# A fused attention and gated-MLP kernel: the second tile's keys loaded in halves, integers compared without a cast, zero products on TensorE before its register loads

## The chip, the cores and the metric

The kernel runs on one core of one Trainium2 chip. The time is device microseconds of one execution. Each run gives the time of the whole execution, and one profiled execution gives a trace whose span is a little shorter than that execution's time. The engines are TensorE (PE, with PEld for its weight loads), VectorE (DVE), ScalarE (ACT), GpSimd (POOL) and SyncE (SP, which here only issues DMAs). A name with a q (PEldq, SPq) is an engine's sequencer.

## The reference

```python
# attention: batch 2, 8 heads, 768 positions, 64 values a head; n_global = 8, n_local = 96
scores = scale * np.matmul(q, k.transpose(0, 1, 3, 2))
rel = pos[:, None] - pos[None, :]
is_global = pos[None, :] < int(n_global)
is_local = (rel >= 0) & (rel < int(n_local))
keep = is_global | is_local
dist = np.where(is_global & ~is_local, float(n_local), np.abs(rel))
scores = np.where(keep, scores - slopes[:, None, None] * dist, -1e9)
a = softmax(scores);  x = np.matmul(a, v)          # then (B, S, 512)
# first gated block: causal convolution of 5 taps as the gate
gate = sigmoid(conv(x, conv_w));  x = (gate * (x @ w_val)) @ w_out
# second gated block: width 1024, centred convolution of 3 taps as the gate
h = relu(x @ w_in);  out = (h * sigmoid(conv(h, conv_w2))) @ w_out2
```

`n_global` and `n_local` are 64-bit integers in memory. `w_out` of the first block and `w_in` of the second are multiplied once, on TensorE, and used as one matrix.

## The kernel before, in words

The queries are worked through in 12 tiles of 128 (two batches of six). A tile's scores are taken against its own 128 keys and the 128 before it, in whose unused columns the global keys are copied. Per tile TensorE makes the scores (line 461) in two halves, heads 0 to 3 and heads 4 to 7; each half uses two of four score banks, so a tile's first half needs the banks that the first half of the tile before it has left, and its second half those of the other half. DVE adds the bias and finds the least value of each head ("least", line 472, one instruction and one short read of the accumulator per head); ACT takes the exponential (line 477); POOL and DVE scale by the reciprocal of the sum (lines 488 to 501); TensorE transposes the result by the identity ("turn", line 528) into the single bank `t`, ACT or DVE copies it out (lines 532 and 538), and TensorE multiplies by the values (line 553). The weights come in 64-bit form through `raw` buffers and are rebuilt as 32-bit numbers by ACT, POOL and DVE (lines 262 to 272); their products and the gated blocks follow, beside the later attention tiles and after them.

The work within the two arms of a branch is planned ahead: a list scheduler (`Plan`) with costs and ring buffers writes out the order of each engine, and the engines keep to it. What stands before the branch is written by hand, in `attention_gated_mlps` (lines 852 to 864): the integers `li`, the first tile's keys and queries `k0` (two halves, one on ACT's queue, one on SP's) and its values `v0` are loaded; every engine loads the integers from memory into its own registers (line 860); DVE turns `li` into floats (`lf`, line 371) and makes the first mask from them (lines 374 to 376). The registers decide the branch of line 957; the arm for small windows is the one that runs. The first things in that arm are the first tile's scores on TensorE, the biases `b` of the eight heads on DVE and POOL (lines 383 and 385), and on SP the load of the second tile's keys and queries (`kq`, 512 KB, line 434). SP's DMA issues stand in one queue, eight DMAs may be under way before an issue waits for an earlier one to land, and each load after the first few waits for its buffer.

Of the kernel before, what the change touches and what calls it, by code (L numbers as in the profile page):

```python
# [9 lines left out]
F32 = mybir.dt.float32  # L10
# [5 lines left out]
PSUM = bass.MemoryType.PSUM  # L16

P = 128
NB, NH, S, D = 2, 8, 768, 64
DM = NH * D  # L20
DFF = 1024
NPAIR = NH // 2
# [5 lines left out]
GW = 32  # L28
# [11 lines left out]
RAWS, MBUFS, HBUFS, Z2BUFS, PBUFS, PTBUFS, KQBUFS, VBUFS = 3, 2, 6, 3, 11, 4, 3, 4  # L40
EARLY = -5.0
LANDING = 2.4
# [184 lines left out]
def dma_us(kb):  # L227
    return max(0.4, kb / 385.0)
# [121 lines left out]
def scratch(c):  # L350

    x = [c.x[:, d, XP:] for d in range(NC1)]
    c.rel, c.w, c.d = (x[d][:, 0:WIN] for d in range(3))
    c.key, c.far, c.d0 = (x[d][:, 4 * P : 5 * P] for d in range(3))


def positions(c):

    nc = c.nc
    nc.gpsimd.iota(c.rel, pattern=[[-1, WIN]], base=P, channel_multiplier=1, allow_small_or_imprecise_dtypes=True)  # L360
    nc.gpsimd.iota(c.key, pattern=[[1, P]], base=0, channel_multiplier=0, allow_small_or_imprecise_dtypes=True)
    nc.gpsimd.affine_select(
        out=c.rel, in_=c.rel, compare_op=ALU.is_ge, fill=BIG, base=P, pattern=[[-1, WIN]], channel_multiplier=1
    )


def first_mask(c):

    nc = c.nc
    lf = c.small.tile([P, 2], F32, name="lf")  # L370
    nc.vector.tensor_copy(lf, c.li[:, :, 0])
    c.ng, c.nl = ng, nl = lf[:, 0:1], lf[:, 1:2]
    rel, w = c.rel[:, P:], c.w[:, P:]
    nc.vector.tensor_scalar(c.far, c.key, ng, BIG, ALU.is_ge, ALU.mult)
    nc.vector.scalar_tensor_tensor(w, rel, nl, c.far, ALU.is_ge, ALU.mult)
    nc.vector.scalar_tensor_tensor(c.d0, rel, nl, w, ALU.min, ALU.add)
# [29 lines left out]
        pl.any(head_ways(c, WIN, lambda h=h: c.B[:, h, :], d, h), [], ["d"], [("B", h)])  # L406


def fast_attention(c, ap):

    nc, ident, pl = c.nc, c.ident, c.plan
# [3 lines left out]
    def tiles_of(tag, shape, n):  # L415
        return pl.ring(n, lambda: ap.tile(shape, F32, tag=tag, bufs=n, name=tag))

    kqr, vr = tiles_of("kq", [P, NPAIR, 2, P], KQBUFS), tiles_of("v", [P, 2, 4, D], VBUFS)
    pr_, ptr, sts = tiles_of("p", [P, WIN], PBUFS), tiles_of("pts", [P, 2, 2, P], PTBUFS), tiles_of("st", [P, 3, NH], 3)
    gl = ap.tile([P, NPAIR, GW], F32, name="gl")  # L420
    kq, vs = {}, {}

    def keys(t, pr, what):
        return c.first[0][:, pr, what] if t == 0 else kq[t].t[:, pr, what]

    def vals(t, h):
        return c.first[1][:, h // 2, h % 2] if t == 0 else vs[t].t[:, h // 4, h % 4]
# [1 line left out]
    def load(t):  # L429
        b, i = tiles[t]  # L430
        if t == 0:
            return
        kq[t], vs[t] = kqr.new(), vr.new()
        pl.add("SP", dma_us(512), lambda: nc.sync.dma_start(kq[t].t, c.kq[b, i]), [kq[t]], [], [("kq", t)], delay=LANDING)
        src = c.v[b, i * P : (i + 1) * P].rearrange("s h d -> s (h d)")
        pl.add(
            "SP", dma_us(256), lambda: nc.sync.dma_start(vs[t].t.rearrange("p a h d -> p (a h d)"), src),
            [vs[t]], [], [("v", t)], delay=LANDING,
        )
# [4 lines left out]
    for t in range(nt):  # L444
        b, i = tiles[t]
# [3 lines left out]
        nk = len(js) * P  # L449
        st, p = sts.new(), {}  # L450
        load(t)
        for half in range(2):
            s = [c.ring["s"].new() for z in range(2)]

            def scores(half=half, s=s, js=js, t0=t):
                for pr in (2 * half, 2 * half + 1):
                    for n, j in enumerate(js):
                        for z in range(2):
                            hs = slice(z * D, (z + 1) * D)
                            out = s[z].t.rearrange("p (a w) -> p a w", w=WIN)[:, pr % 2, n * P : (n + 1) * P]  # L460
                            nc.tensor.matmul(out, keys(t0, pr, 1)[hs], keys(j, pr, 0)[hs], start=True, stop=True)  # L461
# [44 lines left out]
                )  # L506

        def first_keys(t=t, i=i):
            r = (c.first[0] if t == 0 else kq[t].t)[:, :, 0, 0:GW]
            a, z = (gl, r) if i == 0 else (r, gl)  # L510
            nc.gpsimd.tensor_scalar(a, z, 1.0, 1.0, ALU.mult, ALU.mult)

        if i == 0:
            pl.add("POOL", 0.4, first_keys, held(kq, [t]), [("kq", t)], ["gl"])
        elif i < NT - 1:
            pl.add("POOL", 0.4, first_keys, held(kq, [t]), ["gl"], [("kq", t)])
# [315 lines left out]
def attention_gated_mlps(ctx, tc, kq, v, nn, w_val, conv_w, w_out, w_in2, w_out2, out):  # L832
    nc = tc.nc
    c = Ctx()
# [11 lines left out]
    k0 = c.x[:, :, XP + 2 * P : XP + 4 * P].rearrange("p n (t s) -> p n t s", t=2)  # L846
    v0 = c.x[:, :, XP + 5 * P : XP + 6 * P].rearrange("p a (h d) -> p a h d", d=D)
    c.first = k0, v0
    c.li = c.small.tile([P, 2, 2], I32, name="li")
    one = c.small.tile([P, 1], F32, name="one")  # L850
    c.ident = c.const.tile([P, P], F32, name="ident")
    with tc.manual_schedule():
        nc.sync.dma_start(c.li.rearrange("p n t -> p (n t)"), c.nn.to_broadcast([P, 4]))
        nc.scalar.dma_start(k0[:, 0:2], kq[0, 0, :, 0:2])
        nc.sync.dma_start(k0[:, 2:4], kq[0, 0, :, 2:4])
        nc.scalar.dma_start(v0, v[0, 0:P].rearrange("s (a h) d -> s a h d", a=4))
        scratch(c)
        positions(c)
        nc.vector.memset(one, 0.0)
        _, (glo, ghi, llo, lhi) = nc.values_load_multi_w_load_instructions(c.nn)  # L860
        nc.scalar.activation(one, one, AF.Exp)
        nc.gpsimd.memset(c.x[:, :, 0:XP], 0.0)
        make_identity(nc, c.ident)
        first_mask(c)
# [9 lines left out]
    def arm(fast):  # L874
        with ExitStack() as es:
# [42 lines left out]
            if fast:  # L918
                masks(c, ap)
                attention = fast_attention(c, ap)  # L920
                next(attention)
                n0 = len(pl.work)
# [78 lines left out]
```

## Time and profile before

| | |
|---|---|
| median of 3 runs | 288.72 us (288.35 to 290.06) |
| the profiled execution's own time | 289.12 us |
| its span in the trace | 286.9 us |
| TensorE, DVE, ACT, POOL busy | 94%, 83%, 65%, 33% of the span |
| first product of TensorE | 4.88 us after the span's start |

The busy shares are means over the whole span. The change touches its first part, so the timeline of the first 20 us is read on its own. A row of the timeline gives the start, the duration, the engine, the line, the tiles, and in brackets how long the engine had been idle and what released it. A product of 32-bit numbers on TensorE shows as two instructions, so a count of 16 there is eight products.

### The profile page before, as it was taken

The page shows a single profiled execution, that of the slowest core. Times are in us where ns is not written, and L with a number is a line of the kernel's source. Part 1 is how long each engine was busy: PE and PEld are TensorE (multiplying, and loading weights), DVE is VectorE, ACT ScalarE, POOL GpSimd, SP SyncE. Part 2 cuts the span into 40 slices and gives each one's busy share as a digit, 9 for nine tenths or more (in the row PEclk, how much of TensorE's full clock was granted, in tenths as well). Part 3 has the DMA queues.
Part 4 walks back from the last instruction along what each step waited for, and adds up shares of the span by engine and source line. Part 5 has one row for each costly group of instructions (what it writes and reads, how often), then busy time and mean ns, then how long its engine had stood idle before and what let it go on. Part 6 is the DMA issues. An engine that isn't in the chain of part 4 may idle for free.

```text
span 286.9 us, 5416 instructions
## 1 busy us (share of the span) xinstructions
PE 270.1 (94%) x1832; PEld 227.9 (79%) x1832; DVE 238.6 (83%) x607; ACT 187.2 (65%) x468; POOL 95.4 (33%) x208
## 2 busy tenths in 40 slices
PE   2689799999999999999999999999999999999993
PEld 2567556564557998999999999988999988899882
DVE  3899999999999999999899999999985654356600
ACT  2899798967677879775688554894464354445510
POOL 4555557445554405563443310320512000003000
PEclk9999999999999999999999999999999999999999
DMA  4985756645634111023510000010000011000112
GB/s 133 344 322 143 239 197 213 251 138 169 216 108 148 48 65 58 9 75 93 170 43 0 2 0 0 1 39 38 37 2 0 0 73 39 37 0 2 39 73 85
DMA packets 10276, 26.17 MB, mean 91 GB/s; under 512 B 1408, under 2 KB 2688, under 8 KB 10240
## 3 DMA queue, kind: packets, MB, share of 16 engines
q1 hardware_dynamic: 9440, 25.22, 26.3%
q10 hardware_dynamic: 800, 0.52, 0.6%
q8 instruction: 16, 0.26, 0.4%
q14 instruction: 20, 0.16, 0.2%
HBM read 22.59 MB, written 3.15 MB: 90 GB/s over the span
## 4 chain that ended last, share of the span: by engine, by line
PE 73%; DVE 15%; POOL 3%; issue 3%; ACT 3%; POOLq 1%; DVEq 0%; ACTq 0%
PE s L244 8%; PE s L245 8%; PE s L243 8%; PE f L243 7%; PE f L245 7%; PE f L244 7%; PE s L461 4%; PE x L553 4%; PE t L528 4%; DVE p L472 3%; DVE z L671 2%; PE t L243 2%; PE t L245 2%; PE x L245 2%; PE x L244 2%
## 5 line engine op out<-in xcount | busy, mean ns | idle before, releaser
L477 ACT ACTIVATE p<-p,st 128x256 f32<-128x256 f32 (+1 forms) x96 | 46.1, 483 | 8.0 <-DVE st L472 6.4
L671 DVE SCALAR_TENSOR_TENSOR z<-h,cw,z 128x384 f32<-128x384 f32 x64 | 39.9, 630 | 12.6 <-ACT z L666 10.9
L673 ACT ACTIVATE z<-z 128x384 f32<-128x384 f32 (+2 forms) x48 | 25.2, 524 | 26.2 <-DVE z L671 25.5
L671 DVE SCALAR_TENSOR_TENSOR z<-x,cw,z 128x400 f32<-128x400 f32 (+1 forms) x64 | 39.6, 643 | 0.2
L244 PE MATMUL s<-w,g 128*128 128x512 f32 (+1 forms) x104 | 39.2, 377 | 0.0
L245 PE MATMUL s<-w,g 128*128 128x512 f32 (+1 forms) x104 | 39.2, 377 | 0.0
L243 PE MATMUL s<-w,g 128*128 128x512 f32 (+1 forms) x104 | 39.1, 376 | 0.0
L501 POOL TENSOR_SCALAR p<-p,st 128x256 f32<-128x256 f32 (+1 forms) x50 | 32.5, 660 | 11.0 <-DVE st L491 8.7
L528 PEld LDWEIGHTS t<-ident,p 128*128 128x128 f32 x176 | 19.8, 141 | 16.6 <-issue 5.0
L528 PE MATMUL t<-ident,p 128*128 128x128 f32 x176 | 28.7, 282 | 4.1 <-ACT pts L532 2.1
L319 PE MATMUL f<-w,w 128*128 128x512 f32 x64 | 30.8, 602 | 0.0
L472 DVE CUSTOM_DVE_ANT_0 p<-s,B 128x256 f32<-128x256 f32 x80 | 30.5, 410 | 0.0
L243 PE MATMUL f<-gg,Wh 128*128 128x400 f32 (+1 forms) x80 | 27.7, 347 | 0.0
L245 PE MATMUL f<-gg,Wl 128*128 128x400 f32 (+1 forms) x80 | 27.0, 338 | 0.0
L244 PE MATMUL f<-gg,Wh 128*128 128x400 f32 (+1 forms) x80 | 27.0, 338 | 0.0
L461 PE MATMUL s<-kq 64*128 64x128 f32 x320 | 25.7, 292 | 0.8 <-DVE st L472 0.7
L461 PEld LDWEIGHTS s<-kq 64*128 64x128 f32 x320 | 21.5, 194 | 4.9 <-issue 2.6
L667 POOL TENSOR_SCALAR z<-h,cw 128x384 f32<-128x384 f32 x10 | 8.9, 887 | 45.9 <-DVE z L671 31.0
L264 POOL TENSOR_SCALAR raw<-raw 128x512 f32<-128x512 f32 x24 | 18.3, 764 | 16.7 <-ACT m L262 14.1
L236 DVE TENSOR_TENSOR g<-z,g 128x384 fp32r<-128x384 f32 x32 | 17.8, 562 | 5.9 <-ACT g L234 5.9
L245 PEld LDWEIGHTS s<-w,g 128*128 128x128 f32 x104 | 19.5, 188 | 3.8
L244 PEld LDWEIGHTS s<-w,g 128*128 128x128 f32 x104 | 19.6, 188 | 2.8
(117 smaller groups left out, 633.6 us busy)
## 6 DMA issues: line engine op xcount, KB each, us to landing
raw<-in_moe_w_out_dram SPq DMA_DIRECT2D x12, 512.0 KB, 3.4
kq<-in_kq_dram SPq DMA_DIRECT2D x11, 512.0 KB, 4.4
raw<-in_moe_w_in_dram SPq DMA_DIRECT2D x8, 512.0 KB, 5.3
v<-in_v_dram SPq DMA_DIRECT2D x11, 256.0 KB, 3.6
out_dram<-o SPq DMA_DIRECT2D x11, 256.0 KB, 2.0
raw<-in_moe_w_val_dram SPq DMA_DIRECT2D x4, 512.0 KB, 3.5
v<-in_v_dram SPq DMA_DIRECT2D x8, 64.0 KB, 2.8
x<-in_kq_dram ACTq DMA_DIRECT2D x1, 256.0 KB, 4.0
```

Of the source, the lines that this page charges most:

```text
L243: nc.tensor.matmul(out, lh, rh, start=first, stop=False)
L244: nc.tensor.matmul(out, lh, rl, start=False, stop=False)
L245: nc.tensor.matmul(out, ll, rh, start=False, stop=last)
L264: "POOL", pool_us(n), lambda: nc.gpsimd.tensor_scalar(whole(), whole(), 0.0, 1.0, ALU.mult, ALU.mult),
L319: nc.tensor.matmul(ps.t, big["wot"].t.bitcast(F32)[:, e, cs], big[wi].t.bitcast(F32)[:, e, :], start=e == 0, stop=e == 3)
L461: nc.tensor.matmul(out, keys(t0, pr, 1)[hs], keys(j, pr, 0)[hs], start=True, stop=True)
L472: nc.vector.tensor_tensor_reduce(w.t[:, :nk], sc, bias, -QKSCALE, 3.0e38, ALU.add, ALU.min, st.t[:, 0, h : h + 1])
L477: nc.scalar.activation(w.t[:, :nk], w.t[:, :nk], AF.Exp, bias=st.t[:, 0, h : h + 1], scale=-1.0, accum_out=st.t[:, 1, h : h + 1],)
L501: nc.gpsimd.tensor_scalar(w.t[:, :nk], w.t[:, :nk], st.t[:, 2, h : h + 1], 1.0, ALU.mult, ALU.mult)
L528: nc.tensor.transpose(o[:, z, n, :], p[2 * pr + z].t[:, n * P : (n + 1) * P], ident)
L671: nc.vector.scalar_tensor_tensor(z(), src(k), w()[:, k : k + 1], z(), ALU.mult, ALU.add)
L673: pl.add("ACT", act_us(n), lambda: nc.scalar.activation(z(), z(), AF.Tanh, scale=0.5), bufs, [], [token])
```

## The change

Four things are changed. The second tile's keys and queries get a buffer of their own, `k1`, outside the ring `kq`, which loses one of its three buffers and takes `k1` as every third; `k1` is loaded in two halves ahead of the branch, the first on ACT's queue where `v0` was, the second on SP's queue behind SP's register loads, with `v0` after it. DVE's cast is gone, and the masks read the low words of the integers as their scalars. TensorE gets three products of constant zeros, 512, 512 and 128 columns wide, into a bank that nothing reads, ahead of its register loads. The planner still counts the load of tile 1 as SP's work, so the order of the arms stays.

```diff
 def first_mask(c):
-    lf = c.small.tile([P, 2], F32, name="lf")
-    nc.vector.tensor_copy(lf, c.li[:, :, 0])
-    c.ng, c.nl = ng, nl = lf[:, 0:1], lf[:, 1:2]
+    c.ng, c.nl = ng, nl = c.li[:, 0, 0:1], c.li[:, 1, 0:1]
...
+def idle(c, out, widths):
+    for n in widths:
+        zeros = [c.nc.const_aps.tensor(0.0, [P, w], F32) for w in (P, n)]
+        c.nc.tensor.matmul(out[:, :n], *zeros, start=True, stop=True)
...
-    kqr, vr = tiles_of("kq", [P, NPAIR, 2, P], KQBUFS), tiles_of("v", [P, 2, 4, D], VBUFS)
+    kqr, vr = tiles_of("kq", [P, NPAIR, 2, P], KQBUFS - 1), tiles_of("v", [P, 2, 4, D], VBUFS)
+    kqr.n, more = KQBUFS, kqr.make
+    kqr.make = lambda turn=iter(range(99)): more() if next(turn) % KQBUFS else c.second
...
         kq[t], vs[t] = kqr.new(), vr.new()
-        pl.add("SP", dma_us(512), lambda: nc.sync.dma_start(kq[t].t, c.kq[b, i]), [kq[t]], [], [("kq", t)], delay=LANDING)
+        if t == 1:
+            pl.add("SP", dma_us(512), lambda: None, [kq[t]], [], [("kq", t)], delay=LANDING)
+        else:
+            pl.add("SP", dma_us(512), lambda: nc.sync.dma_start(kq[t].t, c.kq[b, i]), [kq[t]], [], [("kq", t)], delay=LANDING)
...
+    c.second = k1 = c.const.tile([P, NPAIR, 2, P], F32, name="k1")
...
-        nc.scalar.dma_start(v0, v[0, 0:P].rearrange("s (a h) d -> s a h d", a=4))
+        nc.scalar.dma_start(k1[:, 0:2], kq[0, 1, :, 0:2])
         scratch(c)
         positions(c)
         nc.vector.memset(one, 0.0)
+        with tc.tile_pool(name="pw", bufs=1, space=PSUM) as pw:
+            idle(c, pw.tile([P, 512], F32, name="idle"), [512,512,128])
         _, (glo, ghi, llo, lhi) = nc.values_load_multi_w_load_instructions(c.nn)
+        nc.sync.dma_start(k1[:, 2:4], kq[0, 1, :, 2:4])
+        nc.sync.dma_start(v0, v[0, 0:P].rearrange("s (a h) d -> s a h d", a=4))
```

On TensorE, from the register loads to the first tile's scores, the order before (with the semaphores that an instruction waits for; DMAHW is a DMA's, the others are engines'):

```order
L860 TENSOR_LOAD in_n_dram_ptr
L860 TENSOR_LOAD in_n_dram
L957 ISA
L957 REGISTER_ALU x3
L957 COMPARE_AND_BRANCH
L461 MATMUL s<-x 128x128 [waits DMAHW0_49]
L461 MATMUL s<-x 128x128 x3
L461 MATMUL s<-x 128x128 [waits DMAHW2_49]
L461 MATMUL s<-x 128x128 x3
```

And with the change:

```order
L411 MATMUL idle<-const-float32-0.0 128x512 x2
L411 MATMUL idle<-const-float32-0.0 128x128
L876 TENSOR_LOAD in_n_dram_ptr
L876 TENSOR_LOAD in_n_dram
L975 ISA
L975 REGISTER_ALU x3
L975 COMPARE_AND_BRANCH
L474 MATMUL s<-x 128x128 [waits DMAHW0_49,PE_49]
L474 MATMUL s<-x 128x128 x3
L474 MATMUL s<-x 128x128 [waits DMAHW2_49]
L474 MATMUL s<-x 128x128 x3
```

The three products stand ahead of the register loads, and the first scores also wait for TensorE's own earlier work.

On TensorE, the second tile's scores and the first turn behind them, before:

```order
L461 MATMUL s<-x,kq 128x128 [waits DMAHW4_49,DVE_49]
L461 MATMUL s<-x,kq 128x128 [waits DVE_49]
L461 MATMUL s<-kq 128x128 x2
L461 MATMUL s<-x,kq 128x128 x2
L461 MATMUL s<-kq 128x128 x2
L461 MATMUL s<-x,kq 128x128 [waits DVE_49] x2
L461 MATMUL s<-kq 128x128 x2
L461 MATMUL s<-x,kq 128x128 x2
L461 MATMUL s<-kq 128x128 x2
L528 MATMUL t<-ident,p 128x128 [waits DVE_49,Pool_49]
```

And with the change (`k_71` is `k1`):

```order
L474 MATMUL s<-x,k_71 128x128 [waits DMAHW3_49,DVE_49]
L474 MATMUL s<-x,k_71 128x128 [waits DVE_49]
L474 MATMUL s<-k_71 128x128 x2
L474 MATMUL s<-x,k_71 128x128 x2
L474 MATMUL s<-k_71 128x128 x2
L474 MATMUL s<-x,k_71 128x128 [waits DMAHW4_49,DVE_49]
L474 MATMUL s<-x,k_71 128x128 [waits DVE_49]
L474 MATMUL s<-k_71 128x128 x2
L474 MATMUL s<-x,k_71 128x128 x2
L474 MATMUL s<-k_71 128x128 x2
L541 MATMUL t<-ident,p 128x128 [waits DVE_49,Pool_49]
```

The first half of the scores waits for one DMA and for DVE, the second half for another DMA and for DVE; before, the first half waited for the whole tile. The turn still stands behind both halves.

On SP, from the start to the arm's first loads, before:

```order
L853 DMA li<-in_n_dram 128x4
L855 DMA x<-in_kq_dram 128x2x256
L860 TENSOR_LOAD in_n_dram_ptr
L860 TENSOR_LOAD in_n_dram
L957 ISA
L957 REGISTER_ALU x3
L957 COMPARE_AND_BRANCH
L434 DMA kq<-in_kq_dram 128x1024
L291 DMA raw<-in_moe_w_in_dram 128x1024
L437 DMA v<-in_v_dram 128x512
L282 DMA cwr<-in_conv_w_dram 128x88
```

And with the change:

```order
L867 DMA li<-in_n_dram 128x4
L869 DMA x<-in_kq_dram 128x2x256
L876 TENSOR_LOAD in_n_dram_ptr
L876 TENSOR_LOAD in_n_dram
L877 DMA k_71<-in_kq_dram 128x512
L878 DMA x<-in_v_dram 128x4x128
L975 ISA
L975 REGISTER_ALU x3
L975 COMPARE_AND_BRANCH
L291 DMA raw<-in_moe_w_in_dram 128x1024
L450 DMA v<-in_v_dram 128x512
L282 DMA cwr<-in_conv_w_dram 128x88 [waits DMAHW0_49]
```

Two loads stand ahead of the branch. The load of tile 1 is gone from the arm, and what is behind it in the arm keeps its order.

## Rows read from the trace of the kernel before

**Rows 1.** The page: span; engines' busy time; granted clock by slice; chain's shares.

```profile
span 286.9 us, 5416 instructions
...
PE 270.1 (94%) x1832; PEld 227.9 (79%) x1832; DVE 238.6 (83%) x607; ACT 187.2 (65%) x468; POOL 95.4 (33%) x208
...
PEclk9999999999999999999999999999999999999999
...
PE 73%; DVE 15%; POOL 3%; issue 3%; ACT 3%; POOLq 1%; DVEq 0%; ACTq 0%
```

**Rows 2.** Chain that ended last, in order of time (start us, us, what).

```profile
9.04 3.79 PE s L461 x32
...
19.80 0.66 PE t L528 x4
```

**Rows 3.** Timeline, 0 to 17 us (start us, us, engine, line [idle before <-releaser]).

```profile
1.25 0.63 ACTq L856 DMA_DIRECT2D x<-in_v_dram  x1
...
4.04 0.17 DVE L371 CAST lf<-li 128x2 f32<-128x2 int32 x1 [3.18 <-DMA li<-in_n_dram]
4.33 0.29 DVE L374 TENSOR_SCALAR x<-x,lf 128x128 f32<-128x128 f32 x1
...
4.88 2.08 PE L461 MATMUL s<-x 64*128 64x128 f32 x16 [4.88 <-DMA x<-in_kq_dram]
...
5.33 0.34 SPq L434 DMA_DIRECT2D kq<-in_kq_dram  x1
...
6.57 0.28 DVE L472 CUSTOM_DVE_ANT_0 p<-s,b 128x128 f32<-128x128 f32 x1
...
7.20 0.28 DVE L472 CUSTOM_DVE_ANT_0 p<-s,b 128x128 f32<-128x128 f32 x1
...
9.21 0.26 DVE L472 CUSTOM_DVE_ANT_0 p<-s,b 128x128 f32<-128x128 f32 x1
...
10.82 0.65 ACT L262 ACTIVATE w<-raw 128x512 f32<-128x512 f32 x1
...
12.16 0.28 DVE L498 TENSOR_SCALAR p<-p,st 128x128 f32<-128x128 f32 x1
...
13.29 0.42 DVE L538 COPY pts<-t 128x256 f32<-128x256 f32 x1 [0.85 <-PE t L528]
...
14.15 1.16 PE L461 MATMUL s<-kq 64*128 64x128 f32 x16
...
16.50 0.41 DVE L472 CUSTOM_DVE_ANT_0 p<-s,B 128x256 f32<-128x256 f32 x1
```

**Rows 4.** Register loads of line 860 (ns min/median/max, first and last start).

```profile
L860 PEldq TENSOR_LOAD <-in_n_dram_ptr x1: 949/949/949, 0.8 to 0.8; - x1
...
L860 PEldq TENSOR_LOAD <-in_n_dram x1: 2023/2023/2023, 1.8 to 1.8; - x1
...
L860 SPq TENSOR_LOAD <-in_n_dram x1: 1175/1175/1175, 3.4 to 3.4; - x1
```

**Rows 5.** The branches of line 957 on TensorE's sequencer, same columns.

```profile
L957 PEldq COMPARE_BRANCH  x2: 93/1728/3362, 4.6 to 279.9; - x2
```

**Rows 6.** Timeline of TensorE at its last product.

```profile
281.78 0.28 PE L245 MATMUL s<-w,g 128*128 128x256 f32 x1
```

**Rows 7.** Products of line 461 in 4 to 13 us (ns min/median/max).

```profile
L461 PE MATMUL s<-x,kq x16: 417/417/579, 9.0 to 12.0; 64*128 64x128 f32 x16
```

**Rows 8.** Products of line 461 in 14 to 15 us.

```profile
L461 PE MATMUL s<-kq x14: 272/272/373, 14.1 to 14.9; 64*128 64x128 f32 x14
```

**Rows 9.** Timeline of TensorE: two products of 512 columns.

```profile
39.23 1.88 PE L319 MATMUL f<-w,w 128*128 128x512 f32 x4
```

**Rows 10.** DMAs issued at 5.3, 5.8 and 7.2 us (last: us to landing).

```profile
kq<-in_kq_dram SPq DMA_DIRECT2D x1, 512.0 KB, 3.6
...
raw<-in_moe_w_in_dram SPq DMA_DIRECT2D x1, 512.0 KB, 4.3
...
kq<-in_kq_dram SPq DMA_DIRECT2D x1, 512.0 KB, 5.3
```

More of the change, by code (lines that the diff above doesn't have):

```diff
@@ L421, in fast_attention, with key_tile @@
     kq, vs = {}, {}
+    kqr.n, more = KQBUFS, kqr.make
+    kqr.make = lambda turn=iter(range(99)): more() if next(turn) % KQBUFS else c.second
     def keys(t, pr, what):
-        return c.first[0][:, pr, what] if t == 0 else kq[t].t[:, pr, what]
+        return key_tile(t)[:, pr, what]
+    def key_tile(t):
+        return c.first[0] if t == 0 else kq[t].t
     def vals(t, h):
@@ L508, in first_keys @@
         def first_keys(t=t, i=i):
-            r = (c.first[0] if t == 0 else kq[t].t)[:, :, 0, 0:GW]
+            r = key_tile(t)[:, :, 0, 0:GW]
             a, z = (gl, r) if i == 0 else (r, gl)
```

## The prediction

> **What bounds the kernel now.** I read the page first: TensorE is busy for 94% of the span and holds 73% of the chain that ended last [rows 1]. That is a mean. The change touches only the first microseconds, where no product runs before 4.88 us, so the stage is read next, from the chain in order of time and from the timeline. There the chain runs through DVE's list and through one stretch of TensorE: the second tile's 32 score instructions, 9.04 to 12.83 us, then the first turn [rows 2]. On the timeline DVE starts with the cast at 4.04, which the landing of the integers released, and has two stands after it. One is the branch. The other is 0.85 us before the copy of line 538 at 13.29, released by TensorE's turn [rows 3]. The turn stands in TensorE's order behind all the scores of tile 1, and those started at 9.04. The trace names DVE for that start, but the bank's last reader had begun at 7.20 and taken 0.28 [rows 3]; the keys, issued at 5.33, landed 3.6 us later, at 8.93 [rows 3, 10]. So the keys of tile 1 hold DVE's copy, by way of TensorE's list.
>
> [...] A half of a tile's scores costs 3.79 / 2 = 1.9 us at the lower level [rows 2] and 1.16 at the upper (the row at 14.15) [rows 3].
>
> **The change, part by part.**
>
> *The cast.* Cast and the hand-over to the next instruction take 4.33 - 4.04 = 0.29 us [rows 3]. The first mask operation can take the cast's place, since the landing of the integers stays what it is. DVE's mask follows it step by step, and POOL's first bias waits for the same mask, so both move: -0.29. What the mask instructions cost with integer scalars no row shows. The nearest row that reads these integers is the cast itself, 0.17 us. The bounds are therefore 0 and 0.17 for each of six instructions, 1.0 in all. I take 0, because the number and shape of the instructions stay; the upper end goes into the range.
>
> *The keys in halves.* The first half takes the place of `v0` on ACT's queue at 1.25, with the same bytes. The second half is issued on SP behind its register loads, which end at 3.4 + 1.18 = 4.6 [rows 4], and so lands at 8.2 to 8.9, with 3.6 us as for the whole tile and 4.3 as for the load behind it [rows 10]. The first half of tile 1's scores then waits for its bank alone: 7.48 - 0.29 = 7.2. At the lower level it ends at 9.1. The second half needs the banks of heads 4 to 7, whose last reader ends at 9.47 - 0.29 = 9.2 [rows 3], later than the keys. It ends at 9.2 + 1.9 = 11.1 at the lower level or 10.4 at the upper, and a turn of two products adds some 0.5. DVE is free for the copy at 12.16 + 0.28 - 0.29 = 12.15 [rows 3]. In both cases the copy no longer waits: -0.85. What is late next is DVE's own list, which the chain follows from there until TensorE takes over at 19.80 [rows 2].
>
> *What the moved loads push.* SP now issues two loads before its branch and one fewer after it. The weights `raw`, first in the arm now, go out at 4.6 + 0.34 + 0.63 (an issue of keys, one of `v0`) + 0.73 (4.6 to 5.33, the branch) = 6.3 instead of 5.8 [rows 3, 10]. With 4.3 us they land at 10.6, and ACT would take them at 10.82 - 0.29 = 10.5 [rows 3]: at most 0.1, and ACT is not on the chain there. The third tile's keys, 7.2 + 0.5 + 5.3 = 13.0, are due at 14.15 - 1.14 = 13.0 [rows 3, 10]. This cover is used up: 0.1 more and it shows. `v0` itself is first read by the value products behind the third tile's scores; its cover is several microseconds.
>
> *The zero products.* At the upper level two products of 512 columns take 1.88 us [rows 9], so the third, a quarter as wide, some 0.24: 2.1 in all, and 4.2 at the lower. From 0.8 us, when TensorE's sequencer is free [rows 4], they end at 2.9 or 5.0. The first scores start at 4.88 now; behind products that end at 5.0 their first half (2.08 / 2) is done at 6.1, before DVE's first "least", due at 6.57 - 0.29 = 6.28 [rows 3]. So the products cost nothing as long as the register loads behind them start on time; the cover left is 0.2 us. If they raise the clock the scores of tiles 0 and 1 get shorter, but DVE's list covers them, as the sum above shows: 0 as well.
>
> TensorE's sequencer does run ahead of its products: it was at the last branch at 279.9 us, while the last product began only at 281.78 [rows 5, 6]. That speaks for register loads that do not wait. But that branch took 3362 ns, the first one 93 [rows 5]; it may have stood until the products were through, and a load could do the same. [...]
>
> **The sum:** -0.29 - 0.85 = -1.14 us. The profiled execution took 289.12, so 287.98; it stood 0.40 above the median of 288.72, so the forecast for the median is 287.6. That is 0.4% less. One per cent, 2.9 us, is about what a measurement of this kernel tells from no change, so the forecast is no change, on its fast side.
>
> **The rivals.**
>
> *The register loads wait for the products (slower).* Then they start at 5.0, take 0.95 + 2.02 [rows 4] and end at 8.0. From there to the first product it is 0.9 (3.8 to 4.7, the branch's 4.6 and 93 ns) [rows 4, 5], and half the first scores take 1.05: the first "least" comes at 9.9 instead of 6.57, +3.3. The stand of 0.85 still goes, since the keys are there: +2.45, 291.2 us. With products at the upper level it is 2.1 less, 289.1. It decides by where TensorE's two load rows start: near 0.9 or at the products' end; from 0.8 + 2.1 on it costs. For it the slow branch, against it the sequencer's lead. Chance 0.12.
>
> *The clock falls back (or does not rise) in the new stands.* Now the engine works from 9.04 without a stop to the first turns and is at the upper level by 14.15. With the change the same work is spread over 4.9 to 11.6 with stands between the halves and one of about 1 us before 12.6. If the level is low when the third tile comes, its two halves take 2 x (1.9 - 1.16) = 1.5 us more; the first scores of that tile would come at 13.0 + 1.9 = 14.9 against DVE's need at 16.50 - 1.14 = 15.4 [rows 3], so 0.5 is covered and 1.0 is not: 288.6, and up to 289.5 if the turns and outputs between them lengthen too. [...] Chance 0.17.
>
> *The keys are not the end of the wait, or the gain is given back later.* If the second half landed 1 us later than reckoned, or the third tile's keys took over, most of the 0.85 would stay and the cast's 0.29 remain: 288.4. For it the used-up cover of the third tile's keys. Chance 0.08.
>
> *More than reckoned.* Where TensorE's list starts earlier, later waits of ACT and POOL on turns may shrink too, another 0.5 to 1: 286.8. Against it: DVE's list is full behind 13.29. Chance 0.05.
>
> **How the numbers follow.** The forecast has 0.58. The predicted time is its value, 287.6. The range reaches from 286.9 (most of the larger gain left out) to 289.5 (the clock's fall, the later stands, the price of integer scalars, and the lower part of the held loads): it leaves out about 0.2. All cases but extremes of the first and last rival lie within 1% of 288.72: 0.04 for faster, 0.91 for the same, 0.05 for slower.
>
> **What would show it.** Right: DVE's first mask operation at about 4.04; no stand before the copy at some 12.15; tile 1's first scores at about 7.2; TensorE's load rows near 0.9 us and its first scores before 5.2. Wrong: load rows behind the products; scores of the third tile at 417 ns; a first mask operation longer than 0.29; the start of DVE's copy 1.1 us earlier, but a span that is not.

## The result: 0.7% slower, and a low clock on TensorE from 12 to 22 us

| | before | changed |
|---|---|---|
| median of 19 runs each | 289.19 us (288.33 to 290.44) | 291.8 us (288.55 to 292.5) |
| the profiled execution's own time | 289.12 us | 292.06 us |
| its span | 286.9 us | 290.1 us |
| its mean granted TensorE clock | 0.998 | 0.980 |

The ratio of the times is 1.0067, with a 95% interval of 1.005 to 1.0085. The forecast was 287.6 us, the sum for the profiled execution 287.98; that execution took 292.06, which is 4.08 more. Not every execution of the changed kernel lost as much: 14 of the 19 ran at a mean granted clock of 0.979 to 0.981 and took 291.5 to 292.5 us, two at 0.985 to 0.987 took 290.4 to 290.5, and three at 0.990 to 0.994 took 288.6 to 289.9. Executions of before spread too: eight of its 19 took 290.0 to 290.4 and the others 288.3 to 289.3, and where the clocks of more of them are on record, beside the experiments, all are at 0.997 or more. The ratios below leave out executions more than 1.5% above the fastest of the same kernel, so beside a ratio stand the median and the clocks of all executions.

The page of the changed kernel, the lines that answer to [rows 1]:

```profile
span 290.1 us, 5432 instructions
...
PE 276.2 (95%) x1838; PEld 230.9 (80%) x1838; DVE 238.8 (82%) x606; ACT 187.1 (65%) x468; POOL 96.4 (33%) x208
...
PEclk9859999999999999999999999999999999999998
...
PE 71%; DVE 14%; ACT 5%; issue 2%; DMA 2%; POOL 2%; ACTq 0%; DVEq 0%; POOLq 0%
```

TensorE is busy for 6.1 us more, of which the six zero-product records are 4.18 (next rows); DVE is busy for the same time. The clock's line has an 8 and a 5 in its second and third slices (7.3 to 21.8 us), where before it had a 9 in all. The timeline of the changed kernel from the start to the copy, against [rows 3]:

```profile
0.77 4.18 PE L411 MATMUL idle<-const-float32-0.0 128*128 128x512 f32 x6 [0.77 <-PEq L993]
...
3.91 0.29 DVE L372 TENSOR_SCALAR x<-x,li 128x128 f32<-128x128 f32 x1 [3.05 <-DMA li<-in_n_dram]
...
4.78 0.33 SPq L877 DMA_DIRECT2D k<-in_kq_dram  x1
...
5.06 1.32 PE L474 MATMUL s<-x 64*128 64x128 f32 x16
...
6.84 0.58 PE L474 MATMUL s<-x,k 64*128 64x128 f32 x3 [0.46 <-DVE st L485]
...
10.13 0.44 PE L541 MATMUL t<-ident,p 128*128 128x128 f32 x2
...
11.72 0.41 DVE L551 COPY pts<-t 128x256 f32<-128x256 f32 x1
...
11.88 0.67 ACT L262 ACTIVATE w<-raw 128x512 f32<-128x512 f32 x1 [1.45 <-DMA raw<-in_moe_w_in_dram]
...
12.19 0.69 PE L541 MATMUL t<-ident,p 128*128 128x128 f32 x2 [1.62 <-DVE pts L551]
...
14.15 0.80 PE L474 MATMUL s<-k,kq 64*128 64x128 f32 x4 [1.28 <-DMA kq<-in_kq_dram]
...
21.50 1.00 PE L566 MATMUL x<-pts,x 128*64 128x128 f32 x8
```

Up to 11.72 us the change does more than was forecast: the copy starts 1.57 earlier than the 13.29 of before, with no stand. But TensorE, which now has the second tile's scores behind it at 10.2, stands for 1.62 us before the second turn and for 1.28 before the third tile's scores. Those start at 14.15, the very time of before, and wait for their keys. The chain of waits of the changed kernel from there (start us, us, what):

```profile
8.01 6.01 DMA kq<-in_kq_dram
...
14.15 2.08 PE s L474 x16
16.23 0.62 PE t L541 x2
...
18.52 2.01 PE s L474 x16
20.53 1.06 PE t L541 x4
```

Where before DVE's list led until TensorE took over at 19.80 [rows 2], TensorE alone leads from 14.15 to 21.59, without a pause, and half a tile's scores take 2.08 us instead of the 1.16 of the row at 14.15 [rows 3]. The windows of the changed kernel (start:end and length in us, busy us of PE, PEld, DVE, ACT and POOL, granted clock, DMA share, GB/s):

```profile
10.00:11.00 1.00, 0.57 (x4) 0.21 (x3) 1.00 (x7) 0.42 (x2) 0.62 (x2) 1.00 0.82 183
11.00:12.00 1.00, 0.00 (x0) 0.00 (x0) 1.00 (x6) 0.12 (x1) 0.68 (x3) 1.00 0.98 310
...
12.00:14.00 2.00, 0.69 (x2) 0.29 (x2) 1.91 (x10) 2.00 (x8) 0.99 (x2) 0.50 1.03 372
14.00:16.00 2.00, 1.85 (x16) 1.82 (x16) 1.20 (x5) 1.99 (x9) 1.10 (x3) 0.50 0.97 339
...
20.00:22.00 2.00, 2.00 (x16) 1.45 (x16) 0.66 (x2) 0.66 (x4) 0.50 (x2) 0.50 0.47 102
22.00:23.00 1.00, 1.00 (x10) 0.64 (x8) 1.00 (x5) 0.38 (x1) 0.48 (x1) 0.87 0.96 385
```

The granted clock is at 0.50 from 12 us to a little past 22. It fell at the end of TensorE's stand of 1.62 us (10.57 to 12.19), and came back after eight microseconds of work without a pause. The third tile's scores took a median of 417 ns from 14.15 to 16 us, which the prediction had named as a sign that it was wrong. Over 20 to 22 us DVE is busy for 0.66 of 2.00: it waits for TensorE now.

### The profile page after: what moved, and what is told of

It is laid out like the page before. It is cut to its first block, busy times and chain, and to the rows that moved or that the text cites. A ratio compares the mean times of both kernels' runs of the same rounds, so it can differ in the third digit from the quotient of the medians.

```text
span 290.1 us, 5432 instructions
## 1 busy us (share of the span) xinstructions
PE 276.2 (95%) x1838; PEld 230.9 (80%) x1838; DVE 238.8 (82%) x606; ACT 187.1 (65%) x468; POOL 96.4 (33%) x208
## 4 chain that ended last, share of the span: by engine, by line
PE 71%; DVE 14%; ACT 5%; issue 2%; DMA 2%; POOL 2%; ACTq 0%; DVEq 0%; POOLq 0%
PE s L244 8%; PE s L245 8%; PE s L243 8%; PE f L243 7%; PE f L245 7%; PE f L244 7%; PE x L566 4%; PE t L541 4%; PE s L474 4%; DVE p L485 3%; DVE z L684 2%; PE t L243 2%; ACT p L490 2%; PE x L245 2%; PE t L245 2%
## 5 line engine op out<-in xcount | busy, mean ns | idle before, releaser
L684 DVE SCALAR_TENSOR_TENSOR z<-h,cw,z 128x384 f32<-128x384 f32 x64 | 39.9, 631 | 12.6 <-ACT z L679 10.9
L514 POOL TENSOR_SCALAR p<-p,st 128x256 f32<-128x256 f32 (+1 forms) x50 | 33.1, 671 | 12.0 <-DVE st L504 10.7
L541 PE MATMUL t<-ident,p 128*128 128x128 f32 x176 | 29.7, 289 | 4.8 <-DVE pts L551 2.5
L541 PEld LDWEIGHTS t<-ident,p 128*128 128x128 f32 x176 | 20.5, 145 | 17.0 <-issue 4.9
L236 DVE TENSOR_TENSOR g<-z,g 128x384 fp32r<-128x384 f32 x32 | 17.9, 564 | 5.9 <-ACT g L234 5.9
L245 PEld LDWEIGHTS s<-w,g 128*128 128x128 f32 x104 | 19.5, 188 | 3.8
L244 PEld LDWEIGHTS s<-w,g 128*128 128x128 f32 x104 | 19.6, 188 | 2.8
L243 PEld LDWEIGHTS s<-w,g 128*128 128x128 f32 x104 | 19.5, 188 | 2.8
L797 DVE SCALAR_TENSOR_TENSOR z<-z,h 128x384 f32<-128x384 f32 x32 | 17.8, 559 | 4.0 <-ACT z L686 3.6
```

Of the source, the lines that this page charges most:

```text
L236: "DVE", dve_us(n), lambda: nc.vector.tensor_tensor(lo(), src(), hi().bitcast(F32), ALU.subtract),
L243: nc.tensor.matmul(out, lh, rh, start=first, stop=False)
L244: nc.tensor.matmul(out, lh, rl, start=False, stop=False)
L245: nc.tensor.matmul(out, ll, rh, start=False, stop=last)
L514: nc.gpsimd.tensor_scalar(w.t[:, :nk], w.t[:, :nk], st.t[:, 2, h : h + 1], 1.0, ALU.mult, ALU.mult)
L541: nc.tensor.transpose(o[:, z, n, :], p[2 * pr + z].t[:, n * P : (n + 1) * P], ident)
```

## Experiments

Two theories. **The clock theory**: the stands that the early keys open on TensorE send its clock to the lower level, and the third and fourth tiles' products, run there, are the loss. **The loads theory**: the moved loads push the third tile's keys and the weights `raw` back, and that takes the gain away. Where a lag is told, it is the start of the same reciprocal on DVE, tile by tile, against the trace of before; the changed kernel's was -0.51 at 15.3 us (in before's time), +2.55 at 19.7, +3.02 at 21.9, and stayed within 0.12 of that up to 116 us.

**e1_filled: the changed kernel, with zero products in the two stands.**

```diff
+FILL = {(0, 0): [512, 256], (0, 1): [512]}      # (tile, pair of heads) of a turn
...
                         nc.tensor.transpose(o[:, z, n, :], p[2 * pr + z].t[:, n * P : (n + 1) * P], ident)
+                idle(c, xp.t, FILL.get((t0, pr), []))
```

Expected:

> The changed kernel with more products of constant zeros on TensorE: 512 and 256 columns behind the first turn and 512 behind the second, so that TensorE does not stand from 10.6 to 12.2 and from 12.9 to 14.1 us. Loads and everything else stay. Theory of the clock (the clock falls to 0.50 in the first of these stands and the work from 14.15 to 22 us at the lower level costs 3 us): the granted clock stays at 1.00, the third tile's scores still start near 14.1, and the time is 288.4 to 289.2 us, 3 us under the changed kernel's 291.8. Theory of the loads (what costs is that the third tile's keys land at 14.0 and the weights at 11.8): as the change, 291.8.

Measured: 289.07 us (12 runs, 288.19 to 292.85), ratio to before 0.9992 (0.9971 to 1.0013). The profiled execution took 288.95 at a clock of 0.996. Its timeline of TensorE:

```profile
10.39 1.46 PE L412 MATMUL x<-const-float32-0.0 128*128 128x512 f32 x4
12.16 0.44 PE L542 MATMUL t<-ident,p 128*128 128x128 f32 x2 [0.32 <-DVE pts L553]
12.44 1.03 PE L412 MATMUL x<-const-float32-0.0 128*128 128x512 f32 x2
13.46 0.49 PE L475 MATMUL s<-k,kq 64*128 64x128 f32 x4
...
17.56 0.66 PE L568 MATMUL x<-pts,x 128*64 128x128 f32 x8
```

From the third tile's first scores to its second value products TensorE now takes 17.56 - 13.46 = 4.10 us; the same instructions, unbroken in both traces, took 21.50 - 14.15 = 7.35 in the changed kernel. The lower level costs 3.25 us there. The lag is -1.59 at 15.3 us and -1.40 at 19.7, so it was the clock that turned gain into loss. (Of the difference of 3.95 us at 19.7 another 0.69 is that in this execution the third tile's keys, issued at 7.99, took 5.3 us instead of 6.0, and its scores began at 13.46 instead of 14.15; the loads themselves were not changed.) But it is -0.58 from 21.9 on, and the chain shows why:

```profile
10.20 9.39 DMA raw<-in_moe_w_in_dram
...
19.61 0.68 ACT w L263
...
20.36 0.68 POOL raw L265
...
21.12 0.20 POOL st L502
```

The third block of weights took 9.39 us to land. ACT and POOL stand in their order behind it, and DVE's reciprocal stands behind POOL. That is 0.8 us for the loads theory, as a second term. And four of the 12 executions were still at 0.991 or 0.992 (289.75 to 290.25) and one at 0.987 (292.85), so the clock may have fallen elsewhere in these; none of them has a trace.

**e2_no_zero: the changed kernel without its three zero products.**

```diff
-        with tc.tile_pool(name="pw", bufs=1, space=PSUM) as pw:
-            idle(c, pw.tile([P, 512], F32, name="idle"), [512,512,128])
```

Expected:

> The changed kernel without the three zero products ahead of the register loads; early keys and the missing cast stay. Theory of the clock: the scores of tiles 0 and 1 run at the lower level, 1.9 us a half, and fill 4.9 to 11.1 us almost without a stand; the clock rises late (after 9 us) and the stand before the third tile's scores is shorter, so it falls less often: 289 to 291. If the clock falls all the same: 291.8. Theory of the loads: the loads are unchanged, so 291.8. That the products themselves hold something up: 289 and the register loads earlier.

Measured: 291.07 us (12 runs, 287.57 to 292.76), ratio 1.0013 (0.9982 to 1.0043); the profiled execution 292.38 at 0.979. Six of the 12 were at 0.979 to 0.981. The scores of two tiles run unbroken from 4.77 to 10.5 there and reach 272 ns at some 9 us; TensorE then stands as in the changed kernel, up to 12.24, and the clock falls at 12 us all the same (0.52 over 12 to 14 us, 0.50 behind). Lag -0.48 at 15.3, +3.06 at 21.9.

```profile
12.24 0.69 PE L541 MATMUL t<-ident,p 128*128 128x128 f32 x2 [1.61 <-DVE pts L551]
```

So the fall does not need the zero products: the early keys are enough. The ratio says little here, since it leaves out five of the 12. Whether the zero products make the fall more frequent (14 of 19 with them, six of 12 without) cannot be told from so few.

**e3_v0_act: the changed kernel, `v0` on ACT's queue again, behind the first half of `k1`.**

```diff
         nc.scalar.dma_start(k1[:, 0:2], kq[0, 1, :, 0:2])
+        nc.scalar.dma_start(v0, v[0, 0:P].rearrange("s (a h) d -> s a h d", a=4))
...
-        nc.sync.dma_start(v0, v[0, 0:P].rearrange("s (a h) d -> s a h d", a=4))
```

Expected:

> The changed kernel with the first tile's values back on ACT's queue, behind the first half of the second tile's keys, so that SP issues one load fewer before its branch. Theory of the loads: the third tile's keys go out 0.7 us earlier, land at 12.6 to 13.2 instead of 14.0, and the time falls by 0.8 to 1.4, to 290.4 to 291.0, if the clock still falls. Theory of the clock: the fall at 12.0 us comes before the third tile's scores in any case, so the granted clock is still 0.50 from about 12 us for some 8 to 10 us and the time stays above 290; only if it does not fall is the time 287.5 to 288.

Measured: 289.52 us (12 runs, 287.62 to 292.51), ratio 1.0015 (0.9984 to 1.0046). In the profiled execution (289.3 at 0.993) the third tile's keys land at 13.12 instead of 14.02, the clock is low, at 0.50, from some 13.5 to 16.9 only, and the lag goes from -1.23 at 15.3 to 0.00 at 21.9. Five of the 12 executions stayed at 0.980 to 0.982 (291.5 to 292.5). Neither theory had forecast the six executions at 288.8 to 289.5. Earlier keys shorten the second stand, and the fall comes later, or not at all (one execution, at 0.997). This ties the theories together: late loads make a stand, and behind the stand the clock is low (0.50 from 13.5 us here). It takes neither away.

**e4_zero_only: the kernel before with the three zero products alone** (the lines that e2_no_zero takes out).

Expected:

> The kernel before with the three zero products alone; its cast and its loads stay. Theory of the clock: the first scores run at the upper level (1.2 instead of 2.1 us), then TensorE stands from 6.3 to 9.0 us for the second tile's keys, longer than the stand in which the clock fell in the changed kernel; the clock falls in or right behind it, and from there it may stay at 0.50 for 8 to 10 us, where the kernel before ran its third tile at the upper level: 289 to 291.5. If the products only help: 288.5. Theory of the loads: 289.2, as before.

Measured: 289.49 us (12 runs, 288.0 to 290.99), ratio 1.0004 (0.998 to 1.0028); all 12 executions at 0.981 to 0.994, where the runs of before beside them were all at 0.997 or more. Timeline of TensorE:

```profile
0.77 4.18 PE L413 MATMUL idle<-const-float32-0.0 128*128 128x512 f32 x6 [0.77 <-PEq L984]
5.06 2.05 PE L468 MATMUL s<-x 64*128 64x128 f32 x16
9.15 0.49 PE L468 MATMUL s<-x,kq 64*128 64x128 f32 x4 [2.04 <-DVE st L479]
...
13.62 2.08 PE L468 MATMUL s<-kq 64*128 64x128 f32 x16
```

and its windows:

```profile
10.20:10.40 0.20, 0.20 (x9) 0.20 (x7) 0.20 (x2) 0.20 (x3) 0.20 (x1) 0.92 1.23 424
10.40:10.60 0.20, 0.20 (x7) 0.20 (x5) 0.20 (x2) 0.20 (x2) 0.12 (x1) 0.50 1.12 405
...
17.20:17.40 0.20, 0.20 (x3) 0.12 (x2) 0.00 (x0) 0.20 (x2) 0.01 (x1) 1.00 1.03 399
```

Here is another stand, of 2.04 us, with the keys loaded whole and no load moved. The clock falls behind it too, at 10.4, when TensorE had been at work again for 1.2 us, and is low up to 17.2. The lag is -0.57 at 15.3 and +0.48 at 21.9. So the zero products alone are enough for a fall as well, and raising the clock early bought little here, where a stand follows (ratio 1.0004). In this trace they did not even raise it in time: the first scores, at 5.06, still took a median of 418 ns, and only those behind the stand ran at 272.

**e5_cast_only: the kernel before without its cast.**

```diff
-    lf = c.small.tile([P, 2], F32, name="lf")
-    nc.vector.tensor_copy(lf, c.li[:, :, 0])
-    c.ng, c.nl = ng, nl = lf[:, 0:1], lf[:, 1:2]
+    c.ng, c.nl = ng, nl = c.li[:, 0, 0:1], c.li[:, 1, 0:1]
```

Expected:

> The kernel before without the cast, nothing else. DVE's first mask operation starts at about 4.0 and its list runs 0.3 to 0.5 us ahead up to 12 us; but its copy at 13.29 still waits for TensorE's turn, which hangs on the second tile's keys, so the lead is eaten there: 289.1, with at most 0.2 off. If the cast's 0.29 were on the path by itself: 288.8. The clock as before, 0.998 or more.

Measured: 289.25 us (12 runs), ratio 0.9995 (0.9969 to 1.0021), clocks 0.997 to 0.999. DVE is 0.28 earlier at 10.9 us and then waits:

```profile
13.61 0.42 DVE L536 COPY pts<-t 128x256 f32<-128x256 f32 x1 [1.04 <-PE t L526]
```

The copy's stand is 1.04 instead of the 0.85 of [rows 3]: with the keys as the end of the wait the cast's time goes into that stand. In this execution the copy came 0.32 later than in before, not earlier: the keys were issued at 5.40 instead of 5.33, the second tile's scores began at 9.17 instead of 9.04, and the turn took 0.69 us instead of 0.49. The interval is wider than the cast's 0.29 us, so the run shows no gain, but could not have told one so small. The first mask operation takes 0.29 us with integer scalars, as it did with floats.

**e6_filled_v0: e3_v0_act and zero products in the two stands** (`FILL = {(0, 0): [512, 512], (0, 1): [128]}`).

Expected:

> The changed kernel with the first tile's values on ACT's queue and the stands of TensorE filled with zero products (512 and 512 columns behind the first turn, 128 behind the second). Theory of the clock alone: granted clock at 1.00 to beyond 20 us, DVE's lead of 1.2 us or more at 15 us is kept to the end, 287.8 to 288.3. Theory that the loads take back what the clock leaves (the third weights' load landed at 19.6 with the filled stands, 17.9 before, and the lead went from 1.4 to 0.6 there): the lead again falls to 0.6 or less at about 20 us, 288.5 to 289.

Measured: 289.09 us (12 runs, 288.01 to 291.2), ratio 0.9994 (0.9962 to 1.0025). Seven executions at 0.996 or more took 288.0 to 289.3, five at 0.982 to 0.994 took 289.65 to 291.2. The lag of the profiled one (289.65) was -1.02 at 15.3 and -0.80 at 21.9, a loss of 0.22 where e1_filled lost 0.82 from 19.7 on. How much of that is `v0`'s place on SP is not shown: e6_filled_v0 had 0.57 less lead to lose, and its third block of weights still landed at 19.3 (issued at 9.77, 9.5 us), against 19.6 in e1_filled and 17.9 in before. At 128 us the lag is still -1.36. Up to the last product that execution lost half of it (this product began at 281.16, before's at 281.78), and the rest behind the last product, where the span ended 6.5 us after its start instead of 5.1. Its granted clock was at 1.00 up to 284 us and at 0.50 only behind the last product, so a mean of 0.994 alone does not show a fall that costs time.

**e7_warm: the kernel before with the three zero products, and three more behind the first tile's scores.**

```diff
+                if t0 == 0 and half == 1:
+                    idle(c, xp.t, [512, 512, 384])
```

**e8_warm_cast: the same without the cast.** Expected of the two:

> The kernel before, its cast and loads as they were, with the three zero products ahead of the register loads and three more (512, 512, 384 columns) between the first and the second tile's scores, so that TensorE does not stand from 6.3 to 9.0 us. Theory of the clock: the clock stays up, the second tile's scores from 9.0 take 2.3 instead of 3.8 us, the turn is ready by 11.9, DVE's stand of 0.85 goes, and since the loads are those of before (third weights at 17.9) most of it is kept: 288.2 to 288.5. If the loads of before are themselves late for a lead: 288.9. If the clock falls all the same: 289.5, as with zero products alone.

> As the run before it in this list, and without the cast. Theory of the clock: both gains stand together, 0.3 and 0.85, 287.9 to 288.2. If the cast gives nothing of its own: as the kernel with the cast, 288.2 to 288.5. If the loads limit: 288.9.

Measured: 288.4 us (ratio 0.9982, 0.9957 to 1.0007) and 288.52 us (0.9965, 0.9941 to 0.999). Filling the stand of e4_zero_only kept the clock up in the profiled execution of e7_warm (0.999), and its lag is -1.06 at 15.3 us and still there at 116 (-1.07). Four and five of 12 executions were at 0.991 to 0.993. The profiled one of e8_warm_cast (289.89) was one of them, and shows the place: a lag of -1.31 at 29.0 us, and then, behind two stands of 0.72 us,

```profile
30.00:31.00 1.00, 1.00 (x14) 0.99 (x14) 0.98 (x4) 1.00 (x5) 0.00 (x0) 0.76 0.81 315
31.00:32.00 1.00, 1.00 (x6) 0.71 (x4) 0.90 (x2) 0.56 (x3) 0.56 (x1) 0.50 0.50 131
```

a second low stretch, up to about 34 us, after which the lag is +0.15. Before has the same two stands, 0.72 and 0.73 us, and passed them at 1.00 in its trace.

**e9_stands: e8_warm_cast, with zero products in those later stands too.** All but the first three go into another unread bank, `fz`.

```diff
+FILL = {(2, 1): [384], (2, 2): [384], (3, 0): [384]}
...
+                if (t0, pr) in FILL:
+                    idle(c, c.psum.tile([P, 512], F32, "f", "fz"), FILL[t0, pr])
```

**e10_stands_late: the same without the first three zero products. e11_change_stands: the changed kernel with the fillings of e1_filled and of e9_stands.** Expected of the three:

> The kernel before without the cast, with the three zero products ahead of the register loads and more of them where TensorE stands: 512, 512 and 384 columns between the first and the second tile's scores, and 384 columns behind each of three later turns (before the stands at about 27.5, 29.3 and 34 us, in which the clock fell in 5 of 12 executions without them). Theory of the clock: no execution with a mean granted clock under 0.996 any more, and the time 287.4 to 288.0, the lead of 1.3 us kept. If the falls do not come from these stands: some executions near 289.5 at a mean clock of 0.992, as without the later products. If the products get in the way of the turns behind them: 288.5 to 289 at a high clock.

> As the run before it in this list, but without the three zero products ahead of the register loads. Theory of the clock: the first scores and the products behind them run at the lower level until about 9 us, the products (3.8 us at that level) end at 10 to 10.7 instead of 9.3 and hold the second tile's scores, which then run at the upper level: DVE's lead at 15 us is 0.3 to 0.9 instead of 1.3, 288.2 to 288.8. If the zero products at the start do nothing: as the run before it.

> The changed kernel with zero products in its stands: 512 and 256 columns behind the first turn, 512 behind the second, and 384 behind each of the three later turns. Theory of the clock: no execution under a mean clock of 0.994, and 288.0 to 288.7. Theory that the loads take the rest back: DVE's lead is 1.4 us at about 19 us and 0.6 at 22 us, so the time stays 0.6 to 0.8 above the kernel with the loads of before and filled stands.

Measured, 12 runs each beside the same 29 of before (median 289.18):

| | median us (all) | ratio (95%) | clocks | lag at 15.3, 21.9, 116 us |
|---|---|---|---|---|
| e9_stands | 288.1 (287.41 to 288.6) | 0.9957 (0.9938 to 0.9975) | 0.995 to 1.000 | -1.25, -1.26, -1.72 |
| e10_stands_late | 289.02 (288.72 to 289.91) | 0.999 (0.9972 to 1.0009) | 0.997 to 0.999 | -0.20, -0.21, -0.21 |
| e11_change_stands | 288.6 (288.15 to 288.9) | 0.9971 (0.9952 to 0.999) | 0.995 to 0.999 | -0.85, -0.26, -0.22 |

e9_stands, in the windows of its trace:

```profile
10.00:12.00 2.00, 1.59 (x24) 1.23 (x21) 2.00 (x12) 2.00 (x8) 1.58 (x6) 1.00 1.02 382
12.00:14.00 2.00, 1.39 (x18) 1.18 (x18) 2.00 (x10) 1.96 (x9) 1.17 (x4) 1.00 1.01 315
14.00:16.00 2.00, 1.85 (x20) 1.16 (x19) 2.00 (x9) 2.00 (x7) 1.38 (x3) 1.00 1.05 399
```

DVE has no idle time in these six microseconds and TensorE's granted clock stays at 1.00. With the stands filled no execution of either kernel was under 0.995: e11_change_stands is 3.2 us faster than the changed kernel by the medians. Ten of the 29 executions of before took 290.0 to 290.6, at clocks of 0.999 or 1.000, so the fallen clock is not their cause; no trace shows one of them. Against the median of the other nineteen, 289.0, e9_stands gains 0.9 instead of 1.1.

Without the three zero products at the start the kernel is 0.9 slower (e10_stands_late against e9_stands). That is more than 288.2 to 288.8, the forecast for e10_stands_late, and it is not the worth of these products by themselves. The filling behind the first tile's scores then takes 3.56 us and ends too late, so that it holds up the second tile's scores itself:

```profile
7.06 3.56 PE L412 MATMUL fz<-const-float32-0.0 128*128 128x512 f32 x6
10.55 0.49 PE L467 MATMUL s<-x,kq 64*128 64x128 f32 x4
```

In e9_stands the same filling starts at 6.33 and takes 2.64, and the scores start at 9.16. A kernel without either of these two was not run with the later stands filled.

The halved keys bring no gain here: e11_change_stands, which has them, is 0.5 slower than e9_stands, which loads the keys whole; eight of the 12 executions of e9_stands are below the lowest of e11_change_stands. The two also differ in `v0`'s queue and in where the first fillings stand. With `v0` on ACT the halved keys did no better: among executions at 0.996 or more e6_filled_v0 has a median of 288.27 (seven) and e8_warm_cast, with whole keys, 287.79 (seven). The traces say where e11_change_stands loses, in the place where e1_filled did:

```profile
10.45 9.34 DMA raw<-in_moe_w_in_dram
...
19.81 0.69 ACT w L263
```

In e9_stands the third block of weights lands at 18.0 (issued at 9.17, 8.8 us). e9_stands is the best version, 1.1 us under before.

## Why the prediction was wrong, step by step

- **The cast** was right for its place: the first mask operation starts at 3.91 and takes 0.29, the integer scalars cost nothing. Alone it shows no gain (e5_cast_only), since the keys end the wait there.
- **The keys in halves** did what was forecast, and early: first scores of the second tile at 6.84 (7.2 forecast), the copy at 11.72 (12.15) without its stand. A gain of 1.57 stood there, against 1.14.
- **The register loads** did not wait for the zero products. That rival is refuted by TensorE's two load rows in the changed kernel, which start where they did [rows 4] and are done at 3.7 us, 1.2 before the products end:

```profile
L876 PEldq TENSOR_LOAD <-in_n_dram_ptr x1: 954/954/954, 0.8 to 0.8; - x1
...
L876 PEldq TENSOR_LOAD <-in_n_dram x1: 1929/1929/1929, 1.8 to 1.8; - x1
```

- **The time of the zero products** was right, 4.18 us against 4.2 for the lower level, at which scores take 417 ns and not 272 [rows 7, 8]. That they take twice as long there as at the upper was an estimate that no row of before shows.
- **"This cover is used up: 0.1 more and it shows"** was about the third tile's keys, put at 13.0. They were issued at 8.01 instead of 7.7 and took 6.0 instead of 5.3:

```profile
kq<-in_kq_dram SPq DMA_DIRECT2D x1, 512.0 KB, 6.0
```

Their scores began at 14.15, 1.15 later than the step had it, which the third rival ("or the third tile's keys took over") had at a chance of 0.08. Some of it is the single execution: in e1_filled, with the same loads, they began at 13.46. The first `raw`, put at 10.6, held ACT until 11.88.
- **The step that failed is the clock, which the sum put at nothing.** It stands in two places. The keys' step ends with "What is late next is DVE's own list, which the chain follows from there until TensorE takes over at 19.80", and the zero products' step with "If they raise the clock the scores of tiles 0 and 1 get shorter, but DVE's list covers them ...: 0 as well." Both counted what earlier and shorter products gain, and not that they end sooner and leave TensorE standing. Either is enough for the fall: the early keys without the zero products (e2_no_zero, a stand of 1.61 us), and the zero products without the early keys (e4_zero_only, 2.04 us). What was late next was TensorE, at the lower level from 14.15 to 21.59, where the clock costs 3.25 us (e1_filled). The rival "The clock falls back (or does not rise) in the new stands" had the mechanism at a chance of 0.17, but with too small a price. It priced two halves of scores at 1.5 and up to 0.9 for what stands between, less a cover of 0.5. Measured from start to start, the halves cost (16.16 - 14.15) - (14.55 - 13.46) = 0.92 each, 1.84 in all, and the turns and value products between them the rest of 3.25, 1.41. The cover of 0.5 was gone, with the keys 1.15 late.

The two terms make up the miss. In before the value products at the end of that stretch start at 18.64:

```profile
16.58 0.44 PE L528 MATMUL t<-ident,p 128*128 128x128 f32 x2 [0.32 <-ACT pts L532]
...
18.64 0.66 PE L553 MATMUL x<-pts,x 128*64 128x128 f32 x8
```

By the forecast that is 17.50 in the changed kernel, and it is 21.50: 4.00 late, of the 4.08 in the whole time. Late keys are 1.15 of it. The other 2.86 is the stretch itself, 7.35 us instead of 18.64 - 14.15 = 4.49, and that is the clock's 3.25 less the short pauses which before had there.

In the changed kernel the granted clock was at 0.50 behind stands of 1.62 and 1.28 us, and in e4_zero_only behind one of 2.04. That before shows no fall after a stand of 2.08 us (6.96 to 9.04) is no evidence against this: the clock had not yet risen then, since the products behind that stand still took 417 ns, and 272 only from 14.1 us [rows 7, 8].

Not settled: why the loads run later with the halved keys. The bytes are the same. Two issues of 0.33 and 0.66 us now stand ahead of SP's branch, so `raw` goes out at 6.61 instead of 5.8 and the keys at 8.01 instead of 7.2, but the keys also took 6.0 us to land instead of 5.3 [rows 10]. The later issue is not all of it: with `v0` back on ACT's queue the third block of weights was issued at 9.64 (e3_v0_act) and 9.77 (e6_filled_v0) instead of 9.27, and landed at 19.5 and 19.3 instead of 17.9. Why these loads take longer stays open. Nor is it settled why before and e7_warm pass their stands of 0.72 us at the upper level in their traces and e8_warm_cast does not in its own.

## What to carry to other kernels

A load that comes earlier can cost time where it lets TensorE run ahead and then stand: look for what the engine does with the time it gains, and price the clock for all that it does while the clock is low (12 to 22 us in the changed kernel), not for one tile. Products of zeros into a bank that nothing reads (or that is overwritten before it is read, as `x` in e1_filled) filled such stands without a loss where they ended before the awaited data (e9_stands, 1.1 us under before); where they ended too late, in e10_stands_late, they held up the scores by 1.4 us. With all the stands of the early stretch filled no execution was under 0.995 (e9_stands, e11_change_stands); with the later ones left open four of 12 were at 0.992 or 0.993 (e7_warm), and three products ahead of the kernel gave nothing alone (e4_zero_only, ratio 1.0004). Read the granted clock of many executions before trusting one trace, since one program ran here at 0.979 to 0.994, and look where in the trace it is low: in e6_filled_v0 it was at 0.50 only behind the last product, where no product is left to slow.

## What the runs showed of the hardware

- The clock fell at the end of a stand (12.0 us in the changed kernel) or 1.2 us behind one (10.4 in e4_zero_only). It was granted at 0.50 from 12.0 to 22.2 us in the changed kernel, through eight microseconds of unbroken 32-bit products (14.15 to 22.2), from 10.4 to 17.2 in e4_zero_only and from 13.5 to 16.9 in e3_v0_act.
- It came up behind some 4 us of zero products at the start in six of the nine traces that have them: the scores behind them took a median of 272 ns, where before they took 418. In the other three (e3_v0_act, e4_zero_only, e8_warm_cast) the median there was still 417 or 418.
- Products whose operands are all zero kept the clock up: with the stands filled by them the granted clock of the profiled executions of e1_filled and e9_stands (means of 0.996 and 1.000) shows no fall before 284 us.
- The column of the granted clock shows 1.00 in the first microseconds, though the durations there are those of the lower level; it tells falls, not the level before the first rise (e4_zero_only: 418 ns at 5.06 us under 1.00, 272 ns from 9.45 us).
- Register loads on TensorE's sequencer ran beside products in flight, at 954 and 1929 ns.
